# Mixture of experts on one core: the copies that take gathered rows apart and put them together move from GpSimd to ScalarE

## The chip, the cores and the metric

The kernel runs on one core of one Trainium2 chip. The metric is the device time of one execution in microseconds (us). Three runs of the kernel before are shown, 661.44, 663.84 and 665.75 us; a change is measured as the time after against the time before on one chip.

## What is computed

The reference is an attention over pooled keys and values, whose output feeds a layer of eight experts. Cut to what matters:

```python
k_p = k.reshape(B, H, Sp, 8, D).mean(axis=3); v_p = ...          # B, H, S, D = 8, 8, 576, 64
out = softmax(q @ k_p.T / 8) @ v_p                               # then x: 4608 tokens x 512
order = argsort(-(x @ w_gate).flatten())                         # 4608 x 8 gate values
for idx in order:                                                # greedy, 576 tokens for each expert
    tok, e = idx // 8, idx % 8
    if assigned[tok] < 0 and counts[e] < 576: assigned[tok] = e; counts[e] += 1
for e in range(8):
    out[assigned == e] = maximum(x[assigned == e] @ w1[e], 0) @ w2[e]     # 512 x 1024, 1024 x 512
```

## The kernel before, in words

**Two parts.** `Attention` takes the first 140 us or so and stores x (the tile `xd`, in DRAM). `experts` then works through the experts one after the other; the change is in this part. The experts are taken in the order in which the routing finds them full, and the routing of expert e+1 runs between the work of expert e.

**One expert.** 576 tokens are four tiles of 128 and one of 64. Products are made in three passes of rounded float32 parts: an operand is split into a high part, which ScalarE (ACT) makes by a copy to `fp32r`, and a low part, which VectorE (DVE) makes by a subtraction. So weights become `w1h`, `w1l` (L1034, L1038) and `w2h`, `w2l` (L1044, L1047), tokens `xh`, `xl` (L1026, L1027). `stage1` (L1064) makes h = x @ w1: first eight output tiles over tokens 0 to 255, then eight over tokens 256 to 575, twelve matmuls each (L1082), into five PSUM buffers `h`. ACT takes each finished tile to `hh` and, in the second half, `hr` (L1087, L1089), and DVE makes `hl` of the same PSUM tile (L1090); a buffer is free when both have read it. `stage2` (L1102) makes four tiles of 128 tokens with 24 matmuls each (L1116) and one of 64 (L1121). ACT copies each to `yt` (L1130, two buffers) or `yh`, and GpSimd (POOL) scatters it to the output by an indirect DMA (L1096).

**Getting an expert's tokens.** When the routing has the row numbers (`rows`, DVE, L740), `gather` (L975) fetches x by indirect DMAs on POOL (L997). For the first expert the tokens are turned by TensorE (PE) (L1058). For the other seven each tile goes through these steps:

- `fetch`: the rows of a tile land in one of the three places of `xa`;
- `split` (L1005): a copy on POOL takes the two 16-bit words of each float32 apart, from `xa` to `xg`, 1024 words on each partition;
- a DMA transpose on SP's queue (L1007) brings them back to `xa`, turned;
- `join` (L1014): a copy on POOL puts the two words together again, to `xg`;
- `xt_joined` (L1017): ACT makes `xh` of it and DVE `xl`.

Since `xa` has three places, tiles 3 and 4 are fetched when tiles 0 and 1 are joined. All fetches, splits and joins of an expert are issued in one stretch when the rows are known; POOL works through its queue in order, and so a scatter issued later waits behind them.

**The routing.** It is a search for the threshold of each expert: DVE makes comparisons (`cmp`, L601), PE counts them (`rt`, L644), DVE reduces, PE folds (L656), DVE compares (`g`, L663), PE spreads the answer (L670), and so on for four rounds, then `close` (L681) finds the rows. These PE instructions stand between the matmuls of the expert at work; PE works in order, so one that waits for DVE holds back the matmuls behind it.

**What sets the order of the work.** `experts` writes one program with a clock of its own, `now`, which counts the time that PE's matmuls should take. `advance` moves it on by the length of each matmul and issues the next step of the routing when the clock has come to it; `later` keeps DVE work until it is due; `turns` and `turn` issue `xt_joined` for tile t when 16 + 1.5 t us have passed on that clock since the rows. The engines keep the order that is written there, but not its times.

In this text the seven gatherings with splits and joins are numbered 1 to 7 by the expert that they are for. Gathering 1 falls into stage 2 of the expert before it, gathering 2 begins at the end of stage 1 of expert 1, and gatherings 3 to 7 begin in the middle of a stage 1.

Of the kernel before, what the change touches and what calls it, by code (L numbers as in the profile page):

```python
# [15 lines left out]
U16 = mybir.dt.uint16  # L16
AF = mybir.ActivationFunctionType
# [907 lines left out]
class Experts:  # L925
# [46 lines left out]
    def rows_of(self, t):  # L972
        return min(128, self.cap - 128 * t)

    def gather(self, rows, turned=False):  # L975

        self.xg = self.buf("xg", [128, 5, 512])
        if not turned:
            for t in range(5):
                self.fetch(rows, t, self.xg[:, t])  # L980
            return
        self.xa = self.buf("xa", [128, 3, 512])
        for t in range(3):
            self.fetch(rows, t, self.xa[:, t])
        for t in range(3):
            self.split(t)
        for t in range(5):
            self.join(t)
            if t < 2:
                self.fetch(rows, t + 3, self.xa[:, t])  # L990
            if t == 2:
                self.split(3)
                self.split(4)

    def fetch(self, rows, t, to):
        n = self.rows_of(t)
# [3 lines left out]
    def split(self, t):  # L1000

        nc = self.nc
        n = self.rows_of(t)
        xs = self.xg[:n, t].bitcast(U16)
        nc.gpsimd.tensor_copy(xs.rearrange("p (s d) -> p s d", s=2),  # L1005
                              self.xa[:n, t % 3].bitcast(U16).rearrange("p (d s) -> p s d", s=2))
        nc.sync.dma_start(self.planes(t), xs, transpose=True)  # L1007

    def planes(self, t):
# [1 line left out]

    def join(self, t):
        n = self.rows_of(t)
        self.nc.gpsimd.tensor_copy(self.xg[:, t].bitcast(U16).rearrange("p (j k s) -> p s j k", j=4, s=2)[:, :, :, :n],  # L1014
                                   self.planes(t).rearrange("p (s j) k -> p s j k", s=2))

    def xt_joined(self, t, later):  # L1017

# [127 lines left out]
def kernel(ctx, tc, q, k, v, wblk, moe_w1, moe_w2, out):  # L1146
# [23 lines left out]
    with ExitStack() as c2:  # L1170
        rows = cst.tile([128, 6], I32, name="lastrows")

        def keep():
            nc.vector.tensor_copy(rows[:, :5], R.rows)
            nc.vector.tensor_copy(rows[:, 5:], R.halves)


        X, flag, ps = experts(c2, tc, g, R, xd, moe_w1, moe_w2, out, A.ident, cap, keep)
        fast, X.scatters, X.fixed = X.scatters, [], True
        with tc.If(flag > 0):  # L1180
            experts_one_by_one(X, R, ps)
            keep()
        X.scatters += fast
        X.put(1, ps, rows, rows[:, 5:])
        for _ in X.stage2(7, rows, rows[:, 5:], range(2, 5)):
            pass


def experts(ctx, tc, g, R, xd, w1, w2, out, ident, cap, keep):
# [3 lines left out]
    nc = tc.nc  # L1193
    wk = ctx.enter_context(tc.tile_pool(name="moe", bufs=2))
    psB = ctx.enter_context(tc.tile_pool(name="psB", bufs=1, space=PSUM))
    X = Experts(tc, wk, psB, xd, w1, w2, out, ident, cap)

    toks, since, pieces, turned = {}, {}, {}, {}
    held, waiting = [], []

    now, dve, ready = 0.0, 0.0, 0.0

    def later(after, t, f):

        waiting.append((now + after, t, f))

    def flush(left=0):
        nonlocal dve
        while len(waiting) > left:
            due, t, f = waiting.pop(0)  # L1210
            f()
            dve = max(dve, due) + t

    def step(e):

        nonlocal now, ready, dve
        p, crit, t, what = held.pop() if held else next(g, (None, 0.0, 0.0, None))
        if p is None:
            return False
        if what == "id":  # L1220

            if p > e or p and pieces[p - 1].l < 8:
                held.append((p, crit, t, what))
                return False
            X.load_1(R.eid, 0, 4 if p else 2)
            eids[p] = R.eid
        elif what == "rows":
            if p and turned[p - 1] < 5:
                held.append((p, crit, t, what))
                return False  # L1230
            X.gather(R.rows, p > 0)
            toks[p] = R.rows, R.halves
            turned[p] = 0
        since[p, what] = now

        now += 0.2
        start = max(dve, now + 0.3)
        ready, dve = start + crit + 0.1, start + t
        return t > 0

    def advance(e, t):

        nonlocal now
        now += t
        while True:
            if waiting and waiting[0][0] <= now:
                flush(len(waiting) - 1)
            elif ready > now or not step(e):
                break

    def due(e, what, t):
        return (e, what) in since and now >= since[e, what] + t

    class Pieces:
# [10 lines left out]
        def next(self, ahead=True):  # L1265
            nonlocal dve
            if self.h == self.l:
                self.up()
            if ahead:
                self.up()  # L1270
            self.low(self.e, self.l)
            self.l += 1
            dve = max(dve, now) + 0.7
# [6 lines left out]
    def turn(e, t, name="tp", bufs=2):  # L1280

        nonlocal now
        if e:
            now = max(now, since[e, "rows"] + 16.0 + 1.5 * t)
            flush(1)
            X.xt_joined(t, later)
        else:
            now = max(now, since[e, "rows"] + 6.0 + 1.3 * t) + 0.45
            flush(1)
            X.xt(t, name, bufs, later)  # L1290
        turned[e] = t + 1
        if (e, t) == (0, 4):
            later(1.0, 0.2, lambda: X.load_2(behind(1)))

    def turns(e, upto, t0):

        nonlocal last
        t = turned.get(e, 5)
        if t < upto and due(e, "rows", 16.0 + 1.5 * t if e else 6.5 + 1.3 * t) and now >= last + 1.4:
            last = now  # L1300
            turn(e, t)

# [4 lines left out]
    while (0, "rows") not in since:  # L1307
        step(0)
# [3 lines left out]
    def behind(i):  # L1312
        nc.vector.tensor_copy(late[:, i:i + 1], eids[0])
        return late[:, i:i + 1]
# [10 lines left out]
    now = dve = -1.0  # L1325
    for t in range(2):
        turn(0, t)
        warm(2)
    flush()
    now, ready, dve = 0.0, 0.0, 1.0  # L1330
    last = 0.0
    for e in range(8):
# [5 lines left out]
        for n, dt in enumerate(X.stage1(later, not e)):  # L1338
            k = n if e else n - 48
            if 0 <= k < 48 and n % 2:  # L1340
                w1.by(4 + (k + 2) // 8)
            if (10 if e else 2) <= n < 96:
                turns(e, 5, n)
            if n == (84 if e else 40):
                for t in range(turned[e], 5):
                    turn(e, t)
            if n >= 64 and n % 2:
                w2.by((n - 70) // 14 if n > 70 else 0)
            if not more and n == 48:
                assert next(g, None) is None  # L1350
                flag = R.suspect()
                keep()
            elif not more and n == 136:
                flag = nc.values_load(flag[0:1, 0:1], min_val=0, max_val=1)
            advance(min(e + 1, 7), dt)
# [9 lines left out]
        if more:  # L1365
            while e + 1 not in toks:
                now = max(now, ready)
# [93 lines left out]
```

## Time and profile before

| | |
|---|---|
| runs shown | 661.44, 663.84, 665.75 us, median 663.84 |
| profiled execution | 658.44 us, of which the span is 656.3 us |
| mean granted TensorE clock | 0.956 of full speed |
| busy in the span | PE 597.4 us (91%), PE weight loads 515.1 (78%), DVE 446.8 (68%), POOL 258.3 (39%), ACT 237.3 (36%) |
| splits on POOL, L1005 | 35, the 28 of 128 partitions 1079 ns each |
| joins on POOL, L1014 | 35, the 28 of 1024 words 1443 ns each |
| indirect DMAs for rows, L997, of seven gatherings | 35, 995 ns each on POOL |
| chain of work that ended last | PE 49%, DVE 17%, POOL 16% of the span |

How to read it: the span runs from the first to the last instruction, and times in the timeline are counted from its start. A row of the timeline or of the groups names the line, the engine, the operation and its tiles, and in brackets how long the engine sat idle before it and what ended that. PE is busy for most of the time, so what counts is the time in which it is not, and the time in which its clock was granted at half speed.

### The profile page before, as it was taken

What the parts mean: (1) busy time and instruction counts of PE and PEld (TensorE: products, weight loads), DVE (VectorE), ACT (ScalarE), POOL (GpSimd) and SP (SyncE); (2) the same over time, 40 slices, a digit from 0 to 9 for tenths busy, and PEclk for the clock granted to TensorE, in tenths of its full rate; (3) what the DMA queues carried; (4) which work ended last, traced back from release to release, by engine and by line L of the source; (5) the groups of instructions that cost most, each with busy time, mean ns of one, the idle gap of its engine ahead of it and who ended that gap; (6) DMA issues with size and microseconds to landing.
All of it is one profiled execution on the core that took longest, in us unless ns stands there. A gap on an engine that the chain in (4) does not pass through costs nothing.

```text
span 656.3 us, 11241 instructions
## 1 busy us (share of the span) xinstructions
PE 597.4 (91%) x4155; PEld 515.1 (78%) x4155; DVE 446.8 (68%) x1149; ACT 237.3 (36%) x554; POOL 258.3 (39%) x289
## 2 busy tenths in 40 slices
PE   7999999976898779889799969997999899999994
PEld 5998989864896479669677967886789679988972
DVE  7677778888877568878974896499649916633400
ACT  7444444432532045134314423342225414524310
POOL 2999995002004710843622371146115522731011
PEclk9999999986999779899989999997999899999998
DMA  9999942125407343527411840283047218414011
GB/s 359 419 423 395 401 156 81 66 81 163 167 1 218 87 168 117 133 73 290 114 39 50 312 97 28 101 282 65 32 146 248 50 48 319 107 50 154 1 36 41
DMA packets 65985, 100.37 MB, mean 153 GB/s; under 512 B 36848, under 2 KB 36864, under 8 KB 63232
## 3 DMA queue, kind: packets, MB, share of 16 engines
q1 hardware_dynamic: 54672, 71.18, 32.3%
q0 software_dynamic: 5920, 18.89, 8.2%
q10 hardware_dynamic: 5328, 9.48, 3.8%
q8 instruction: 35, 0.57, 0.4%
q14 instruction: 30, 0.25, 0.1%
HBM read 72.40 MB, written 18.87 MB: 139 GB/s over the span
## 4 chain that ended last, share of the span: by engine, by line
PE 49%; DVE 17%; POOL 16%; issue 8%; DMA 6%; ACT 1%; SPq 1%; POOLq 0%; another core or an unknown queue 0%; DVEq 0%; ACTq 0%
PE h L1116 20%; PE h L1082 20%; DVE w2l L1047 4%; PE h L1121 3%; POOL t L187 3%; POOL tk L174 3%; DVE hl L1090 2%; DVE ow L574 2%; DMA rawk<-in_k_dram 2%; POOL kblk L178 2%; POOL t L188 2%; POOL vblk L197 2%; POOL tk L175 2%; PE psa L271 1%; DMA xa<-xg 1%
## 5 line engine op out<-in xcount | busy, mean ns | idle before, releaser
L1116 PE MATMUL h<-w2h,hh 128*128 128x512 f32 x256 | 103.6, 405 | 2.9 <-DVE hl L1090 2.6
L1116 PE MATMUL h<-w2h,hl 128*128 128x512 f32 x256 | 104.1, 407 | 0.0
L1116 PE MATMUL h<-w2l,hh 128*128 128x512 f32 x256 | 103.6, 405 | 0.0
L1087 ACT ACTIVATE hh<-h 128x320 fp32r<-128x320 f32 (+1 forms) x128 | 52.6, 411 | 140.6 <-PE h L1082 139.2
L1082 PE MATMUL h<-xh,w1h 128*128 128x320 f32 (+1 forms) x512 | 94.5, 305 | 4.1 <-ACT xh L1026 3.2
L1082 PE MATMUL h<-xl,w1h 128*128 128x320 f32 (+1 forms) x512 | 96.8, 306 | 0.0
L1096 POOL DMA_INDIRECT out_dram<-yt,rows x29 | 29.9, 1030 | 167.6 <-ACT yt L1130 166.7
L1082 PE MATMUL h<-xh,w1l 128*128 128x320 f32 (+1 forms) x512 | 93.5, 304 | 0.2 <-DVE w1l L1038 0.2
L1082 PEld LDWEIGHTS h<-xl,w1h 128*128 128x128 f32 x512 | 79.2, 196 | 9.2 <-issue 9.2
L1082 PEld LDWEIGHTS h<-xh,w1h 128*128 128x128 f32 x512 | 77.4, 194 | 7.9 <-ACT xh L1026 3.7
L1082 PEld LDWEIGHTS h<-xh,w1l 128*128 128x128 f32 x512 | 78.1, 195 | 0.6 <-DVE w1l L1038 0.5
L1130 ACT ACTIVATE yt<-h 128x512 f32<-128x512 f32 x32 | 19.2, 599 | 158.8 <-PE h L1116 97.9
L1090 DVE SCALAR_TENSOR_TENSOR hl<-h,hh 128x320 fp32r<-128x320 f32 (+1 forms) x128 | 56.9, 449 | 21.4 <-ACT hr L1089 13.7
L1027 DVE TENSOR_TENSOR xl<-xg,xh 128x512 fp32r<-128x512 f32 (+1 forms) x35 | 23.3, 665 | 64.3 <-ACT xh L1026 64.3
L997 POOL DMA_INDIRECT xa<-xd,rows x35 | 34.8, 995 | 75.4 <-DVE rows L740 67.3
L271 PE MATMUL psa<-vblk,eT 128*128 128x146 f32 (+3 forms) x400 | 62.0, 302 | 0.0
L1047 DVE TENSOR_TENSOR w2l<-raw,w2h 128x512 fp32r<-128x512 f32 x64 | 58.3, 919 | 2.2 <-ACT w2h L1044 2.1
L1116 PEld LDWEIGHTS h<-w2h,hh 128*128 128x128 f32 x256 | 49.6, 194 | 12.8 <-DVE hl L1090 2.9
L1014 POOL COPY xg<-xa 128x1024 uint16<-128x1024 uint16 (+1 forms) x35 | 46.8, 1348 | 26.8 <-DMA xa<-xg 26.7
L1116 PEld LDWEIGHTS h<-w2h,hl 128*128 128x128 f32 x256 | 49.7, 194 | 9.4
L1116 PEld LDWEIGHTS h<-w2l,hh 128*128 128x128 f32 x256 | 49.8, 195 | 9.1
L271 PEld LDWEIGHTS psa<-vblk,eT 128*128 128x128 f32 (+1 forms) x400 | 52.2, 180 | 1.7 <-issue 0.3
(215 smaller groups left out, 983.6 us busy)
## 6 DMA issues: line engine op xcount, KB each, us to landing
raw<-in_moe_w_dram SPq DMA_DIRECT2D x64, 512.0 KB, 6.7
xd<-xt ACTq DMA_DIRECT2D x36, 256.0 KB, 5.0
rawv<-in_v_dram SPq DMA_DIRECT2D x7, 1280.0 KB, 14.8
rawk<-in_k_dram SPq DMA_DIRECT2D x7, 1152.0 KB, 12.8
rawq<-in_q_dram SPq DMA_DIRECT2D x7, 1152.0 KB, 10.5
rawk<-in_k_dram SPq DMA_DIRECT2D x2, 576.0 KB, 4.4
rawv<-in_v_dram SPq DMA_DIRECT2D x1, 768.0 KB, 7.8
rawq<-in_q_dram SPq DMA_DIRECT2D x1, 640.0 KB, 8.9
```

The source lines that it names most:

```text
L174: eng.tensor_tensor(t1[:, c], src[:, c, :4], src[:, c, 4:], op=OP.add)
L187: eng.tensor_tensor(t1[:, c], src[:, c, :256], src[:, c, 256:], op=OP.add)
L271: self.nc.tensor.matmul(o[h], self.eT[i][:, c, h], self.vblk[b % 4][:, self.BLOCKS[c]:self.BLOCKS[c + 1]], start=(c == cs[0]), stop=(c == ...
L997: self.nc.gpsimd.indirect_dma_start(out=to[:n], out_offset=None, in_=self.xd, in_offset=bass.IndirectOffsetOnAxis(ap=rows[:n, t:t + 1], ax ...
L1014: self.nc.gpsimd.tensor_copy(self.xg[:, t].bitcast(U16).rearrange("p (j k s) -> p s j k", j=4, s=2)[:, :, :, :n], self.planes(t).rearrange ...
L1027: later(0.9, 0.7, lambda: self.nc.vector.tensor_tensor(xl, x, xh.bitcast(F32), op=OP.subtract))
L1047: self.nc.vector.tensor_tensor(self.w2l[:, i], self.raw2[e][:, i], self.w2h[:, i].bitcast(F32), op=OP.subtract)
L1082: nc.tensor.matmul(ps[:, :m], a[:, j, fs], b[:, j, o], start=(n == 0), stop=(n == 11))
L1087: nc.scalar.activation(hh[:, f, o], ps[:, :m], AF.Relu)
L1090: later(0.65, 0.4, lambda f=f, o=o, m=m, ps=ps: nc.vector.scalar_tensor_tensor(hl[:, f, o], ps[:, :m], 0.0, hh[:, f, o].bitcast(F32), op0= ...
L1096: st = nc.gpsimd.indirect_dma_start(out=rows, out_offset=bass.IndirectOffsetOnAxis(ap=idx, axis=0), in_=y, in_offset=None)
L1116: nc.tensor.matmul(ps, a[:, f, o], b[:, f], start=(f == 0 and k == 0), stop=(f == 7 and k == 2))
```

## The change

`split` and `join` become ACT copies (`activation` with `AF.Copy`) of the same words; the DMA transposes stay on SP and the fetches on POOL. `gather` no longer issues everything at once: it hands each split and join to `at`, which keeps it until the program's clock has come to a set time after the rows: splits 0 to 2 at 5.0, 6.3 and 7.6 us, joins 0 to 2 at 11.0, 12.3 and 13.6 us (joins 0 and 1 with the fetches of tiles 3 and 4 behind them), splits 3 and 4 at 16.9 and 18.2 us, joins 3 and 4 at 23.9 and 25.2 us. `advance` issues those that are due before it looks at the routing. `turn` comes 20 + 1.5 t us after the rows where it was 16 + 1.5 t. The first expert, and the second path through the experts that runs only if the routing's own test fails, keep the old fetch.

```diff
-    def gather(self, rows, turned=False):
+    def gather(self, rows, at=None):
...
         for t in range(3):
             self.fetch(rows, t, self.xa[:, t])
-        for t in range(3):
-            self.split(t)
-        for t in range(5):
-            self.join(t)
-            if t < 2:
-                self.fetch(rows, t + 3, self.xa[:, t])
-            if t == 2:
-                self.split(3)
-                self.split(4)
+            at(5.0 + 1.3 * t, lambda t=t: self.split(t))
+        for t in range(2):
+            at(11.0 + 1.3 * t, lambda t=t: (self.join(t), self.fetch(rows, t + 3, self.xa[:, t])))
+        at(13.6, lambda: self.join(2))
+        for t in range(3, 5):
+            at(13.0 + 1.3 * t, lambda t=t: self.split(t))
+        for t in range(3, 5):
+            at(20.0 + 1.3 * t, lambda t=t: self.join(t))
...
-        nc.gpsimd.tensor_copy(xs.rearrange("p (s d) -> p s d", s=2),
-                              self.xa[:n, t % 3].bitcast(U16).rearrange("p (d s) -> p s d", s=2))
+        nc.scalar.activation(xs.rearrange("p (s d) -> p s d", s=2),
+                             self.xa[:n, t % 3].bitcast(U16).rearrange("p (d s) -> p s d", s=2), AF.Copy)
...
-        self.nc.gpsimd.tensor_copy(self.xg[:, t].bitcast(U16).rearrange("p (j k s) -> p s j k", j=4, s=2)[:, :, :, :n],
-                                   self.planes(t).rearrange("p (s j) k -> p s j k", s=2))
+        self.nc.scalar.activation(self.xg[:, t].bitcast(U16).rearrange("p (j k s) -> p s j k", j=4, s=2)[:, :, :, :n],
+                                  self.planes(t).rearrange("p (s j) k -> p s j k", s=2), AF.Copy)
...
+    def at(after, f):
+
+        moves.append((now + after, f))
+
+    def move(until):
+        while moves and moves[0][0] <= until:
+            moves.pop(0)[1]()
...
-            X.gather(R.rows, p > 0)
+            X.gather(R.rows, at if p else None)
...
         now += t
+        move(now)
...
-            now = max(now, since[e, "rows"] + 16.0 + 1.5 * t)
+            now = max(now, since[e, "rows"] + 20.0 + 1.5 * t)
+            move(since[e, "rows"] + (11.0, 12.3, 13.6, 23.9, 25.2)[t])
...
-        if t < upto and due(e, "rows", 16.0 + 1.5 * t if e else 6.5 + 1.3 * t) and now >= last + 1.4:
+        if t < upto and due(e, "rows", 20.0 + 1.5 * t if e else 6.5 + 1.3 * t) and now >= last + 1.4:
```

The instructions change their places. In the rows below, line numbers of the changed kernel are its own: one less than before for the lines behind `gather` that the text names (the split is L1004, the join L1013, the scatter L1095, `yt` L1129). `x3` behind a row stands for three in a row.

POOL in gathering 1, before, from the first join on (`xg<-xa` are joins and splits, `out_dram` scatters):

```order
L1014 COPY xg<-xa 128x2x512
L997 DMA xa<-xd,rows 128x512
L1014 COPY xg<-xa 128x2x512
L997 DMA xa<-xd,rows 64x512
L1014 COPY xg<-xa 128x2x512
L1005 COPY xg<-xa 128x1024
L1005 COPY xg<-xa 64x1024
L1014 COPY xg<-xa 128x2x512
L1014 COPY xg<-xa 128x2x4x64
L1095 MEMSET spacer 1x1
L1096 DMA out_dram<-yt,rows 4608x512
```

POOL there now, from the three first fetches on:

```order
L996 DMA xa<-xd,rows 128x512 x3
L1094 MEMSET spacer 1x1
L1095 DMA out_dram<-yt,rows 4608x512
L1094 MEMSET spacer 1x1
L1095 DMA out_dram<-yt,rows 4608x512
L996 DMA xa<-xd,rows 128x512
L996 DMA xa<-xd,rows 64x512
L1094 MEMSET spacer 1x1
L1095 DMA out_dram<-yt,rows 4608x512
```

The scatters of expert 0's second and third tile now stand between the fetches; before, they stood behind the last join.

ACT at the same place, before (from expert 0's tiles of stage 2 to expert 1's first `xh`):

```order
L1130 ACTIVATE yt<-h 128x512 x3
L1034 ACTIVATE w1h<-raw_2602 128x512 x3
L1130 ACTIVATE yt<-h 128x512
L1034 ACTIVATE w1h<-raw_2602 128x512
L1026 ACTIVATE xh<-xg 128x4x128 x2
L1134 ACTIVATE yh<-h 128x256
L1034 ACTIVATE w1h<-raw_2602 128x512 x2
```

and now, from the third `yt` on (the three first splits stand right ahead of it):

```order
L1129 ACTIVATE yt<-h 128x512
L1033 ACTIVATE w1h<-raw_2602 128x512 x2
L1013 ACTIVATE xg<-xa 128x2x512
L1033 ACTIVATE w1h<-raw_2602 128x512
L1013 ACTIVATE xg<-xa 128x2x512 x2
L1129 ACTIVATE yt<-h 128x512
L1033 ACTIVATE w1h<-raw_2602 128x512
L1004 ACTIVATE xg<-xa 128x1024
L1004 ACTIVATE xg<-xa 64x1024
L1133 ACTIVATE yh<-h 128x256
L1033 ACTIVATE w1h<-raw_2602 128x512
L1025 ACTIVATE xh<-xg 128x4x128 x2
```

All five splits and three joins now stand ahead of the first `xh` on ACT, and so do `yh` and five pieces of `w1h` (four before).

ACT in the middle of expert 3's stage 1, where gathering 4 begins, before:

```order
L1044 ACTIVATE w2h<-raw_4392 128x512 x2
L1087 ACTIVATE hh<-h 128x256
L1044 ACTIVATE w2h<-raw_4392 128x512
L1087 ACTIVATE hh<-h 128x320
L1089 ACTIVATE hr<-h 128x64
L1044 ACTIVATE w2h<-raw_4392 128x512
L1087 ACTIVATE hh<-h 128x320
L1089 ACTIVATE hr<-h 128x64
```

and now:

```order
L1043 ACTIVATE w2h<-raw_4392 128x512 x2
L1004 ACTIVATE xg<-xa 128x1024
L1086 ACTIVATE hh<-h 128x256
L1043 ACTIVATE w2h<-raw_4392 128x512
L1004 ACTIVATE xg<-xa 128x1024
L1086 ACTIVATE hh<-h 128x320
L1088 ACTIVATE hr<-h 128x64
L1004 ACTIVATE xg<-xa 128x1024
L1043 ACTIVATE w2h<-raw_4392 128x512
L1086 ACTIVATE hh<-h 128x320
L1088 ACTIVATE hr<-h 128x64
```

The first split stands ahead of the last `hh` of the first half, and each later split or join between the evictions of two tiles.

More of the change, by code (lines that the diff above doesn't have):

```diff
@@ L973, in rows_of @@
         return min(128, self.cap - 128 * t)
-    def gather(self, rows, turned=False):
+    def gather(self, rows, at=None):
         self.xg = self.buf("xg", [128, 5, 512])
-        if not turned:
+        if at is None:
             for t in range(5):
@@ L1205, in later @@
         waiting.append((now + after, t, f))
+    moves = []
+    def at(after, f):
[3 more added lines that the diff above has]
+            moves.pop(0)[1]()
     def flush(left=0):
```

## The prediction

> **What bounds the kernel now.** I read the busy times of the page first, then PE's waits from 200 us on (us in total, times, the longest), then a table of stretches cut so that each of rows two to eight holds one gathering, 1 to 7.
>
> ```profile
> PE 597.4 (91%) x4155; PEld 515.1 (78%) x4155; DVE 446.8 (68%) x1149; ACT 237.3 (36%) x554; POOL 258.3 (39%) x289
> ```
>
> ```profile
> PE rt L644 <- DVE cmp L601: 13.1, 9, 3.2
> PE rt L670 <- DVE g L663: 9.0, 3, 3.4
> PE rt L656 <- DVE cnt L652: 3.7, 3, 1.3
> PE h L1082 <- ACT xh L1026: 3.2, 1, 3.2
> PE h L1116 <- DVE hl L1090: 2.6, 1, 2.6
> ```
>
> ```profile
> core 0: us, PE busy (x) PEld busy (x) DVE busy (x) ACT busy (x) POOL busy (x), PEclk, DMA share, GB/s
> 191.00:262.00 71.00, 61.81 (x400) 50.52 (x399) 49.30 (x141) 20.31 (x49) 21.39 (x24) 0.90 0.44 133
> 262.00:298.00 36.00, 32.39 (x190) 23.45 (x188) 29.41 (x81) 9.22 (x19) 22.19 (x24) 0.95 0.40 108
> 298.00:359.00 61.00, 56.08 (x380) 48.04 (x380) 46.73 (x117) 21.00 (x50) 22.55 (x25) 0.97 0.40 127
> 359.00:421.00 62.00, 56.18 (x380) 48.14 (x378) 45.91 (x114) 21.00 (x50) 21.89 (x25) 0.97 0.39 124
> 421.00:485.00 64.00, 58.17 (x390) 49.45 (x386) 45.97 (x114) 20.98 (x50) 21.70 (x25) 0.95 0.39 125
> 485.00:543.00 58.00, 54.77 (x341) 47.59 (x337) 37.84 (x82) 20.98 (x50) 22.26 (x25) 0.97 0.42 135
> 543.00:600.00 57.00, 57.00 (x379) 51.39 (x378) 29.73 (x61) 23.33 (x56) 24.21 (x26) 1.00 0.50 156
> ```
>
> PE bounds the kernel. What can be won is PE's idle time and the time its clock is granted at half. Length less PE busy gives 9.2, 3.6, 4.9, 5.8, 5.8, 3.2 and 0 us of idle; length times what PEclk lacks of 1 gives 7.1, 1.8, 1.8, 1.9, 3.2, 1.7 and 0. Together the gatherings lose 16.3, 5.4, 6.8, 7.7, 9.0, 4.9 and 0: **50.1 us is the most that this change can win** in them.
>
> The halved clock follows idle time. Columns here are PE's busy time, the granted clock, DMA share and GB/s:
>
> ```profile
> 271.40:274.80 3.40, 1.66 (x16) 1.00 0.51 95
> 274.80:278.20 3.40, 3.40 (x9) 0.50 0.24 84
> ```
>
> A stretch of 3.4 us in which PE is busy for less than half is followed by one at half clock, which costs 1.7 us. [...]
>
> Why DVE is late shows at 385 us. The rows are the timeline of DVE and POOL and two groups of DVE (ns min/median/max):
>
> ```profile
> 385.32 4.20 DVE L574 TENSOR_TENSOR ow<-oh,wts 128x288 f32<-128x288 bf16 x1
> 385.91 1.37 POOL L1014 COPY xg<-xa 128x1024 uint16<-128x1024 uint16 x1
> 387.19 2.01 POOL L1005 COPY xg<-xa 128x1024 uint16<-128x1024 uint16 x2
> L574 DVE TENSOR_TENSOR ow<-oh,wts x8: 436/1162/4201, 140.0 to 505.8; 128x288 f32<-128x288 bf16 x8
> L1090 DVE SCALAR_TENSOR_TENSOR hl<-h,hh x128: 402/448/492, 164.9 to 621.8; 128x256 fp32r<-128x256 f32 x64, 128x320 fp32r<-128x320 f32 x64
> ```
>
> `ow`, with both inputs in SBUF, takes 4.20 us where its fastest took 0.44, and ends when POOL's copies pause; `hl`, which reads PSUM, never stretches. So a POOL copy holds up DVE's instructions with two SBUF inputs. An indirect DMA alone doesn't:
>
> ```profile
> 371.29 0.95 POOL L997 DMA_INDIRECT xa<-xd,rows  x1 [0.31 <-issue]
> 371.83 0.44 DVE L779 TENSOR_TENSOR lg<-lg,pen 128x288 f32<-128x288 f32 x1
> ```
>
> Gathering 1 has a second loss. The scatters wait behind the joins on POOL, `yt` on ACT waits for a scatter, and `xh`, behind `yt`, lets PE begin expert 1 late:
>
> ```profile
> 203.35 1.01 POOL L997 DMA_INDIRECT xa<-xd,rows  x1 [3.17 <-DVE rows L740]
> 208.77 3.00 POOL L1005 COPY xg<-xa 128x1024 uint16<-128x1024 uint16 x3 [1.89 <-DMA xa<-xd,rows]
> 213.32 1.34 POOL L1014 COPY xg<-xa 128x1024 uint16<-128x1024 uint16 x1 [1.55 <-DMA xa<-xg]
> 230.35 0.60 ACT L1130 ACTIVATE yt<-h 128x512 f32<-128x512 f32 x1 [17.71 <-DMA out_dram<-yt,rows]
> 232.55 0.62 PE L1082 MATMUL h<-xh,w1h 128*128 128x256 f32 x3 [3.24 <-ACT xh L1026]
> ```
>
> **The price of a copy on ACT.** No row shows ACT copying 16-bit words with a stride. The nearest are these (busy us, mean ns):
>
> ```profile
> L447 ACT ACTIVATE j<-i 128x1152 f16<-128x1152 f32 x1 | 1.1, 1147 | 0.0
> L1044 ACT ACTIVATE w2h<-raw 128x512 fp32r<-128x512 f32 x64 | 38.9, 628 | 0.0
> L1005 POOL COPY xg<-xa 128x1024 uint16<-128x1024 uint16 x28 | 29.6, 1079 | 19.7 <-DMA xa<-xd,rows 16.8 <-ACT hr L1089 2.7
> L1014 POOL COPY xg<-xa 128x1024 uint16<-128x1024 uint16 x28 | 40.4, 1443 | 24.5 <-DMA xa<-xg 24.4
> ```
>
> 640 elements more cost 519 ns, so 0.81 ns each, and 1024 words cost 1.04 us. Lower bound: two words at a time, 0.63 us, the price of 512. Upper bound: twice the straight price, 2.1 us, if every strided word is paid double. I take 1.04, on the line between ACT's own two rows, and in a row 0.95, since neighbours overlap by about 0.1. An expert has ten copies, some 10 us; 70 us go from POOL (258 busy) to ACT (237). Over the whole span neither is near full; what matters is who waits behind a copy.
>
> **Gathering 1, step by step.** The first split still waits for the fetch, to 208.77; ACT's three end at 211.65. The first transpose lands about when it did, 213.2. Joins 0 to 2 end at 216.7 with one `yt` and three `w1h` around them. The fetch of tile 4, behind join 1 at 215.8, lands at some 220.1, so split 4, which stands ahead of `xh`, ends at 221.1; `yh`, a `w1h` and two `xh` follow, and PE begins expert 1 at about **223.0** (was 232.55). The scatters no longer stand behind joins, so `yt` finds its buffer. PE's own work of expert 0, without waits for `cmp`, ends at 221 to 222. Left: waits of 0.8 and 1.0 and one halved window, 1.7, together 3.5 of 16.3: **-12.8**.
>
> **Gathering 2** has DVE free and no ACT work near; 0.3 left of 5.4: **-5.1**.
>
> **Gatherings 3 to 5.** Here the change adds a wait. In gathering 4:
>
> ```profile
> 368.70 1.01 POOL L997 DMA_INDIRECT xa<-xd,rows  x1 [7.47 <-DVE rows L740]
> 375.55 3.05 POOL L1005 COPY xg<-xa 128x1024 uint16<-128x1024 uint16 x3 [3.31 <-DMA xa<-xd,rows]
> 372.33 0.39 ACT L1087 ACTIVATE hh<-h 128x256 fp32r<-128x256 f32 x1
> L1087 ACT ACTIVATE hh<-h 128x320 fp32r<-128x320 f32 x64 | 28.0, 438 | 82.0 <-PE h L1082 80.8 <-PE rt L755 1.2
> L1089 ACT ACTIVATE hr<-h 128x64 f32<-128x64 f32 x64 | 14.0, 218 | 0.0
> 380.72 0.39 PE L644 MATMUL rt<-oh,cmp 128*128 128x32 bf16 x9 [1.25 <-DVE cmp L601]
> 385.46 0.18 PE L656 MATMUL rt<-cnt,fold 128*128 128x8 f16 x1 [1.18 <-DVE cnt L652]
> 391.04 0.17 PE L670 MATMUL rt<-g,ones 128*128 128x8 bf16 x1 [3.39 <-DVE g L663]
> ```
>
> The rows take 6.85 us from issue to the first split. The first split stands on ACT ahead of the `hh` that ran at 372.33, so ACT stands still for some 3.3 us from 372.2, and that `hh` goes at 376.5. Behind it: `hl` on DVE (which needs `hh`), and behind `hl` the search. ACT then has eight copies (7.6), eight `hh` with their `hr` (3.6 with overlap) and seven `w2h` (3.7): 14.8 us, while PE makes eight tiles of 1.76 us, 14. So ACT catches up slowly, and the five PSUM buffers, some 7 us of PE, just cover it. DVE ends `cmp` at about 381.5 where PE stands at L644 from 379.47 (380.72 less 1.25): a wait of 2.1 where it was 1.25. The next ones have DVE unstretched: 0.35 at L656 (was 1.18), 0.25 at L670 (was 3.39), 1.2 at the next L644. That makes 3.9, and an even chance of a halved window 0.8: 4.7 left in each, of 6.8, 7.7 and 9.0: **-2.1, -3.0, -4.3**. If the buffers didn't cover ACT, its 3.3 us would fall on PE in each.
>
> **Gathering 6** has no search left, only `hl` late (L1116): 0.5 left of 4.9, **-4.4**. **Gathering 7** lost nothing; the copies beside its evictions **+0.5**. Moving `turn` by 4 us costs nothing, as PE reads those tokens only in the next stage 1, over 20 us on.
>
> Sum: -12.8 - 5.1 - 2.1 - 3.0 - 4.3 - 4.4 + 0.5 = **-31.2 us**; from the profiled 658.44 to 627.2. That execution is 0.8% under the median, so in the median 663.84 - 31.2 = 632.6, **633**.
>
> **Rivals.** *B, no new waits*: the rows land sooner in the changed order, or the buffers swallow ACT's stop (a copy at the lower bound takes 3.3 us of eight off ACT), and 3 x 4.7 = 14.1 more go: 619. For it, the fetch of gathering 1 landed after 5.4 us; against it, every gathering from 3 on took about 7. *C1, strided words cost on ACT what a join costs over a split on POOL*, 1.34 times: 1.4 us, 0.32 more for eight copies in five gatherings (1, 3 to 6), 13 us: 646. *D, DVE isn't freed*: POOL's indirect DMAs, which stay, hold it too. Only gathering 1's order gains, 9.6, less three waits longer by 0.85: 657. The row at 371.83 speaks against it, but only one DMA at a time is seen there. *C2, the slower side: ACT becomes the bound.* At 2.1 us a copy, eight copies cost 8.4 more in the half of stage 1 in which ACT already has 14.8 for PE's 14; with the buffers used up PE waits, 42 us in five gatherings against 31 won: 675. It decides from 31.2 / 40 = 0.78 above 1.04, that is at 1.8 us a copy. [...]
>
> **Chances.** Forecast 0.50, B 0.18, C1 0.13, D 0.09, C2 0.10. A measurement of this kernel, with runs 0.65% apart, can tell about 1%. The forecast, B and C1 are faster by over that, 0.81; D lies at its edge and counts as no change, 0.09; C2 is slower, 0.10. The range goes from B, with 2 us below, to D: 617 to 657.
>
> **What would show it.** Right: `ow` and `cmp` near 0.44 and 0.75 us throughout; no wait of `yt` for a scatter; PE's first stage-1 matmul of expert 1 near 223; the first split on ACT waiting some 3 us for its fetch in gatherings 3 to 6; PE's wait at L644 near 2 us there, those at L656 and L670 nearly gone; copies of 1.04 us. Wrong: stretched DVE instructions beside fetches (D), copies over 1.3 us or PE waiting for an `h` buffer (C1, C2), no wait ahead of the split (B).

## The result, and the profile after

The changed kernel takes **625.18 us** in the median of four runs (620.99 to 627.54), beside 664.8 us of the kernel before on the same chip (661.44 to 667.71). The ratio is **0.940, with a 95% interval of 0.933 to 0.947**. The forecast was 633, in a range of 617 to 657. The profiled execution took 625.91 us, with a span of 624.1 us.

The busy times of the page after:

```profile
PE 585.8 (94%) x4155; PEld 509.4 (82%) x4155; DVE 394.1 (63%) x1149; ACT 305.0 (49%) x624; POOL 175.3 (28%) x219
```

ACT has 68 us more and POOL 83 us less, as the moved copies make them. But DVE, whose 1149 instructions are the same, is busy 53 us less (it was 446.8): what it lost is time in which its instructions were held up. PE's 597.4 became 585.8, because fewer of its matmuls ran at half clock (the mean granted clock went from 0.956 to 0.973).

Of PE's waits from 190 us on, these are left (us in total, times, the longest):

```profile
PE rt L644 <- DVE cmp L601: 4.9, 3, 2.0
PE rt L670 <- DVE g L663: 2.2, 2, 1.1
PE h L1081 <- ACT xh L1025: 2.0, 1, 2.0
PE rt L656 <- DVE cnt L652: 0.8, 1, 0.8
```

In the kernel before they were 13.1, 9.0, 3.2 and 3.7, in this order, and one of 2.6 for `hl` at L1116 is gone. To see where the time came from, both traces are cut at the same places of the program: from the beginning of stage 2 of expert 0 to that of expert 1 (gathering 1), then to the beginning of stage 1 of expert 2 (gathering 2), and then from each stage 1 to the next (gatherings 3 to 6; gathering 7 has 52.05 us in both). The columns are length, PE's busy time, the granted clock, DMA share and GB/s. Before:

```profile
192.26:264.29 72.03, 62.84 (x406) 0.91 0.45 138
264.29:298.05 33.76, 30.15 (x174) 0.95 0.39 101
298.05:359.50 61.45, 56.52 (x383) 0.97 0.39 127
359.50:421.84 62.34, 56.52 (x383) 0.97 0.39 125
421.84:485.26 63.42, 57.59 (x383) 0.95 0.39 123
485.26:542.97 57.71, 54.48 (x338) 0.97 0.42 135
```

After:

```profile
195.91:256.83 60.92, 57.98 (x405) 0.97 0.55 168
256.83:284.79 27.96, 27.96 (x174) 1.00 0.43 110
284.79:342.41 57.62, 54.98 (x382) 1.00 0.43 136
342.41:400.64 58.23, 56.24 (x383) 0.97 0.44 134
400.64:458.16 57.52, 54.98 (x383) 1.00 0.45 135
458.16:510.75 52.59, 52.30 (x339) 1.00 0.47 148
```

Row by row, the gatherings give 11.1, 5.8, 3.8, 4.1, 5.9, 5.1 and 0 us, with unrounded rows 35.9. Stage 1 of expert 0 gives another 1.0 (31.19 to 30.20). Against that, the part ahead of it, which the change doesn't touch, took 161.07 us in the profile before and 165.71 after. In the profiles of the experiments below it ends anywhere from 160.8 to 165.6, so it belongs to the single execution. That takes 4.6 us off the difference, so the two profiled executions are only 32.5 us apart, and the medians 39.6.

DVE's group that stretched most before is even now (ns min/median/max), and `cmp`, up to 4.53 us before, takes 0.762 at most:

```profile
L574 DVE TENSOR_TENSOR ow<-oh,wts x8: 434/449/453, 144.5 to 479.0; 128x288 f32<-128x288 bf16 x8
```

The new wait is there too. First the timeline of gathering 4 on ACT, DVE and PE, then the two groups of copies on ACT (busy us, mean ns):

```profile
358.70 1.06 ACT L1004 ACTIVATE xg<-xa 128x1024 uint16<-128x1024 uint16 x1 [3.55 <-DMA xa<-xd,rows]
360.07 0.42 DVE L1089 SCALAR_TENSOR_TENSOR hl<-h,hh 128x256 fp32r<-128x256 f32 x1 [2.94 <-ACT hh L1086]
364.32 0.39 PE L644 MATMUL rt<-oh,cmp 128*128 128x32 bf16 x9 [1.99 <-DVE cmp L601]
```

```profile
L1004 ACT ACTIVATE xg<-xa 128x1024 uint16<-128x1024 uint16 x28 | 29.5, 1064 | 19.5 <-DMA xa<-xd,rows 18.6 <-DVE pen L777 0.9
L1013 ACT ACTIVATE xg<-xa 128x1024 uint16<-128x1024 uint16 x28 | 38.8, 1395 | 1.0 <-DMA xa<-xg 0.9
```

ACT stands 3.55 us for the fetch (2.94 to 3.25 in gatherings 3, 5 and 6), `hh` comes late, then `hl`, then the search on DVE, and PE waits 1.99 us. A split costs 1.06 us, a join 1.40.

### The profile page after: what moved, and what is told of

Read it like the earlier page. It is cut to its first block, busy times and chain, and to the rows that moved or that the text cites. A ratio compares the mean times of both kernels' runs of the same rounds, so it can differ in the third digit from the quotient of the medians.

```text
span 624.1 us, 11279 instructions
## 1 busy us (share of the span) xinstructions
PE 585.8 (94%) x4155; PEld 509.4 (82%) x4155; DVE 394.1 (63%) x1149; ACT 305.0 (49%) x624; POOL 175.3 (28%) x219
## 4 chain that ended last, share of the span: by engine, by line
PE 71%; issue 10%; DMA 7%; ACT 5%; DVE 3%; POOL 1%; POOLq 0%; another core or an unknown queue 0%; SPq 0%; DVEq 0%; ACTq 0%
PE h L1115 23%; PE h L1081 22%; PE psa L271 8%; PE pss L229 6%; DMA xa<-xd,rows 3%; PE h L1120 3%; PE pse L258 2%; ACT xg L1004 2%; PE rt L258 1%; DMA wblk<-in_moe_w_gate_dram 1%; DMA xg<-xd,rows 1%; PE rt L219 1%; PE rt L644 1%; ACT hh L1086 1%; PE rt L505 1%
## 5 line engine op out<-in xcount | busy, mean ns | idle before, releaser
L1115 PE MATMUL h<-w2l,hh 128*128 128x512 f32 x256 | 101.8, 398 | 0.0
L1115 PE MATMUL h<-w2h,hl 128*128 128x512 f32 x256 | 101.6, 397 | 0.0
L1115 PE MATMUL h<-w2h,hh 128*128 128x512 f32 x256 | 100.6, 393 | 0.3 <-PEq L1179 0.3
L1081 PE MATMUL h<-xl,w1h 128*128 128x320 f32 (+1 forms) x512 | 95.3, 303 | 0.0
L1081 PE MATMUL h<-xh,w1l 128*128 128x320 f32 (+1 forms) x512 | 91.0, 300 | 0.0
L1095 POOL DMA_INDIRECT out_dram<-yt,rows x29 | 29.2, 1006 | 200.0 <-ACT yt L1129 199.6
L1081 PEld LDWEIGHTS h<-xl,w1h 128*128 128x128 f32 x512 | 77.8, 192 | 2.3 <-issue 2.3
L1081 PEld LDWEIGHTS h<-xh,w1l 128*128 128x128 f32 x512 | 76.6, 192 | 0.1
L1129 ACT ACTIVATE yt<-h 128x512 f32<-128x512 f32 x32 | 19.2, 599 | 96.9 <-PE h L1115 62.5
L1115 PEld LDWEIGHTS h<-w2h,hl 128*128 128x128 f32 x256 | 48.2, 188 | 9.0
L1046 DVE TENSOR_TENSOR w2l<-raw,w2h 128x512 fp32r<-128x512 f32 x64 | 43.2, 682 | 5.8 <-ACT w2h L1043 5.8
L1004 ACT ACTIVATE xg<-xa 128x1024 uint16<-128x1024 uint16 (+1 forms) x35 | 36.8, 1064 | 19.7 <-DMA xa<-xd,rows 18.6
```

Source lines behind the costliest of these rows:

```text
L1004: nc.scalar.activation(xs.rearrange("p (s d) -> p s d", s=2), self.xa[:n, t % 3].bitcast(U16).rearrange("p (d s) -> p s d", s=2), AF.Copy)
L1046: self.nc.vector.tensor_tensor(self.w2l[:, i], self.raw2[e][:, i], self.w2h[:, i].bitcast(F32), op=OP.subtract)
L1081: nc.tensor.matmul(ps[:, :m], a[:, j, fs], b[:, j, o], start=(n == 0), stop=(n == 11))
L1095: st = nc.gpsimd.indirect_dma_start(out=rows, out_offset=bass.IndirectOffsetOnAxis(ap=idx, axis=0), in_=y, in_offset=None)
L1115: nc.tensor.matmul(ps, a[:, f, o], b[:, f], start=(f == 0 and k == 0), stop=(f == 7 and k == 2))
L1129: self.nc.scalar.activation(y, ps, AF.Copy)
```

## The experiments

Two theories were set against each other. S: the gain comes from POOL's copies no longer holding up DVE. O: it comes from the new order and times, whichever engine copies. Each kernel is the changed one with the edit shown; times are medians, ratios are against the kernel before on the same chip. Its medians lie between 663.4 and 664.8 us on the chips where times are compared, so times of two chips can be set side by side to within a microsecond or two.

### The new order, but on POOL

```diff
-        nc.scalar.activation(xs..., self.xa[:n, t % 3]..., AF.Copy)
+        nc.gpsimd.tensor_copy(xs..., self.xa[:n, t % 3]...)
```

and the same in `join`.

> The changed kernel with its splits and joins on POOL again, but issued where the plan's clock puts them. Theory S (the gain comes from POOL's copies no longer holding up DVE's instructions with two inputs in SBUF): ow, cmp and w2l stretch again, to 2 us and more, and only what gathering 1 wins by its scatters standing ahead of the joins stays: 645 to 658. Theory O (the gain comes from the new order and times, whatever engine copies): 625 to 630, with PE's waits as in the changed kernel.

Measured: **656.86 us, 0.986 (0.980 to 0.992)**. PE's waits, and a piece of DVE's and POOL's timeline:

```profile
PE rt L670 <- DVE g L663: 13.7, 5, 5.2
PE rt L644 <- DVE cmp L601: 6.5, 6, 1.9
PE rt L656 <- DVE cnt L652: 5.0, 4, 1.8
```

```profile
384.61 4.21 DVE L574 TENSOR_TENSOR ow<-oh,wts 128x288 f32<-128x288 bf16 x1
385.20 1.37 POOL L1013 COPY xg<-xa 128x1024 uint16<-128x1024 uint16 x1
386.48 2.02 POOL L1004 COPY xg<-xa 128x1024 uint16<-128x1024 uint16 x2
```

Theory O falls. With order and times kept, `ow` stands 4.21 us again, DVE is busy 452.2 us for 394.1, PE's waits at the search are 25.2 us for 7.9, and 31.7 of the 39.6 us are gone. The order by itself is worth 7 to 8 (664.12 to 656.86 on this chip).

### The new engine, but in one stretch

```diff
     def at(after, f):
-        moves.append((now + after, f))
+        f()
```

> The changed kernel with every split and join issued at once when the rows are known, as in the kernel before, but on ACT. If the plan's times are needed, ACT stands in its queue at the first split until the fetch lands, then at the joins until the transposes land, then at split 3 until the second fetches land: some 20 us for each gathering, of which the five PSUM buffers cover about 7. PE loses 10 us or more in six gatherings: 680 to 710, slower than the kernel before. If the engine alone matters, 625 to 632.

Measured: **751.32 us, 1.130 (1.124 to 1.136)**, worse than expected. ACT's waits:

```profile
ACT xg L1004 <- DMA xa<-xd,rows: 65.6, 16, 10.1
ACT xg L1013 <- DMA xa<-xg: 25.7, 15, 2.5
```

ACT stood 91 us for fetches and transposes, and the evictions, and all of DVE and PE behind them, stood with it: PE waits 88.7 us at stage 1 for `hl` alone. In the kernel before POOL stood in the same way, 26.7 us for transposes and 17.6 for fetches, but behind its copies stood only fetches and scatters, no evictions. So the engine is what gains, and the times are what makes the engine bearable.

### Copies on POOL that nobody waits for

```diff
         nc.scalar.activation(xs..., AF.Copy)
+        for _ in range(2):
+            self.nc.gpsimd.tensor_copy(self.scr..., self.scr...)
```

and the same in `join`; to make room for the tile `scr`, `yh` has one buffer where it had two. Nothing of the output depends on these copies.

> The changed kernel, and beside each split and join on ACT two copies of 512 words on POOL from a spare tile onto itself (yh has one buffer for two, to make room): about 1 us of POOL for each, 10 us a gathering, which nobody waits for. Theory S: DVE's instructions with two SBUF inputs stretch again beside them (ow, cmp, w2l to 1.5 us and more) and a good part of the 25 us that gatherings 2 to 6 won is lost again: 635 to 650. Theory O: POOL's copies are nobody's business, 625 within 3.

Measured: **629.33 us, 0.949 (0.944 to 0.954)**, 4 us above the changed kernel, with intervals that overlap: unclear by the time, and between the ranges of the two theories. `ow` went to 0.94 us at most. The second form took its words from `ident` with a stride for a split, and put them with a stride for a join:

```diff
+            self.nc.gpsimd.tensor_copy(self.scr...rearrange("p (r s d) -> p r s d", r=2, s=2), self.ident...rearrange("p (d s) -> p s d", s=2)...)
```

> As the run with idle copies on POOL, but each idle copy now takes 512 16-bit words from a constant (ident) with a stride, or puts them with a stride, as the real splits and joins did. In the first run of this kind the idle copies went from a tile onto itself without a stride, cost 4 us, and stretched ow to 0.94 us at most. If the stretch of DVE comes from POOL's copies as such, this run is like that one, 627 to 632, ow under 1 us. If it is the stride that makes POOL hold DVE up for the whole of its copy, ow and w2l go to 2 us and more and the time to 635 to 650.

Measured: **636.54 us, 0.961 (0.953 to 0.969)**, clear of the changed kernel, 11 us above it.

```profile
L574 DVE TENSOR_TENSOR ow<-oh,wts x8: 436/640/1017, 143.8 to 489.5; 128x288 f32<-128x288 bf16 x8
L1053 DVE TENSOR_TENSOR w2l<-raw,w2h x64: 668/685/1268, 182.8 to 588.8; 128x512 fp32r<-128x512 f32 x64
```

The time fell into the range of the second reading, but its sign didn't come: `ow` went to 1.02 us and `w2l` to 1.27, not to 2 and more. DVE was busy 428.7 us for 394.1, and PE waited 9.8 us at L644 for 4.9. So copies that nobody waits for do cost time through DVE, as theory S has it, but these held DVE up for one copy at a time, and they cost a third of what the real copies cost on POOL, although POOL was busy for longer (296.1 us, 259.6 with the real ones). PE's wait for `xh` also grew, from 2.0 to 3.4 us; whether the single `yh` buffer or the copies in front of scatters and fetches did that wasn't separated. The last two experiments look at how long DVE is held up.

### Only the splits, or only the joins, on POOL

The edit of the first experiment, in one of the two places (first in `split`, then in `join`):

```diff
-        nc.scalar.activation(xs..., self.xa[:n, t % 3]..., AF.Copy)
+        nc.gpsimd.tensor_copy(xs..., self.xa[:n, t % 3]...)
```

> The changed kernel with the splits on POOL again (5 of 1.08 us a gathering) and the joins on ACT, at the plan's times. Theory S (POOL's copies hold DVE up): DVE stretches during the splits alone, less than half of POOL's copy time of before; against that ACT no longer stands 3.5 us for the fetch: 625 to 638. If ACT's stop cost more than POOL's splits do, under 622.

> The changed kernel with the joins on POOL again (5 of 1.4 us a gathering) and the splits on ACT, at the plan's times. Theory S: the joins stretch DVE and ACT still stands 3.5 us for the fetch: 635 to 650, above the run with the splits on POOL. If only the splits hold DVE up, 622 to 628.

Measured: splits on POOL **624.81 us, 0.946 (0.937 to 0.954)**, not told apart from the changed kernel; joins on POOL **644.14 us, 0.974 (0.966 to 0.982)**. With the splits on POOL, POOL waits for the fetch in ACT's place (3.37 us in gathering 4), and what could be won by that seems to be paid back by splits beside DVE (PE waits 6.5 us at L644, 4.9 in the changed kernel).

With the joins on POOL, `w2l` has a mean of 914 ns (919 in the kernel before, 682 in the changed one):

```profile
L1046 DVE TENSOR_TENSOR w2l<-raw,w2h 128x512 fp32r<-128x512 f32 x64 | 58.1, 914 | 5.5 <-ACT w2h L1043 5.4
```

The first run, just under what S allowed, tells little, since two effects work against each other in it and were not separated. The second lies in S's range: joins on POOL cost 19 us.

### Every copy twice on ACT

```diff
         nc.scalar.activation(xs..., self.xa[:n, t % 3]..., AF.Copy)
+        nc.scalar.activation(xs..., self.xa[:n, t % 3]..., AF.Copy)
```

and the same in `join`, so that each is written twice to the same place.

> The changed kernel with every split and join on ACT made twice, to the same place: 12 us more of ACT in each gathering, as if a copy cost 2.1 us for a split and 2.8 for a join. This is the rival that ACT becomes the bound. If ACT had no room beside PE, its 9 us more in the half of stage 1 would fall on PE beyond what the five buffers still cover, 5 to 9 us in gatherings 1 and 3 to 6: 650 to 670. If ACT has room, 625 to 635.

Measured: **673.47 us, 1.020 (1.011 to 1.029)**: 9 us above the kernel before, and just above the range expected. PE's waits:

```profile
PE rt L670 <- DVE g L663: 16.6, 4, 4.6
PE rt L644 <- DVE cmp L601: 10.6, 4, 3.2
PE rt L656 <- DVE cnt L652: 9.1, 4, 4.2
PE h L1085 <- DVE hl L1093: 3.9, 4, 1.3
```

ACT's room is as small as the prediction had it, but it is hardly the five buffers that give out: only 3.9 us are spent waiting at stage 1 for `hl`. It is the search, with 36.3. DVE works in order, `hl` stands in front of `cmp`, `cnt` and `g`, and `hl` needs `hh` of the late ACT; PE waits at the three steps of the search.

### The due times later

All due times of gatherings 2 to 7, the turn too, 2.6 us later:

```diff
-            X.gather(R.rows, at if p else None)
+            X.gather(R.rows, (lambda a, f: at(a + LATE * (p > 1), f)) if p else None)
...
-            now = max(now, since[e, "rows"] + 20.0 + 1.5 * t)
+            now = max(now, since[e, "rows"] + 20.0 + LATE * (e > 1) + 1.5 * t)
```

`LATE` is 2.6.

> The changed kernel with the due times of gatherings 2 to 7 (splits, joins and the turn into xh) 2.6 us later, gathering 1 as it is. If what the change left in gatherings 3 to 5 is ACT standing at the first split until its fetch lands (3.55 us in gathering 4, and behind it hh, hl, cmp and PE's 1.99 us at L644), the first split now stands behind one or two more evictions, its wait falls from 3.5 to about 1 us, the three waits at L644 (1.49, 1.99, 1.38 us) go, and the time falls by 3 to 6 us, to 619 to 622. If ACT is the bound there by the sum of its work and not by that stop, the waits only come one tile later and the time stays at 625 within 2.

Measured: **617.73 us, 0.930 (0.926 to 0.934)**, 7.4 us under the changed kernel, more than expected. PE's waits, and what is left of ACT's for the fetch:

```profile
PE h L1081 <- ACT xh L1025: 2.0, 1, 2.0
PE rt L670 <- DVE g L663: 1.2, 3, 0.6
PE rt L644 <- DVE cmp L601: 1.0, 3, 0.3
...
ACT xg L1004 <- DMA xa<-xd,rows: 7.5, 6, 3.6
```

The longest wait left, 3.6 us, is that of gathering 1, which was not moved. In gatherings 2 to 7 the waits for fetches fell from 15.3 to 3.8 us, and PE's at L644 from 4.9 to 1.0. So it was the stop of ACT at the first split that the change had left in gatherings 3 to 5, and not the sum of ACT's work, which is the same here and hides. The run moves joins and turns with the splits, so the stop was not taken away alone. Then PE's single wait for `xh`, in gathering 1:

```diff
+def turn_at(e, t):
+    return 15.0 + 1.5 * t if e == 1 and t < 2 else 20.0 + LATE + 1.5 * t
```

with splits and joins 3 and 4 of gathering 1 2.6 us later.

> The run with gatherings 2 to 7 taken 2.6 us later, and in gathering 1 the turn of tokens 0 to 255 at 15.0 and 16.5 us, ahead of yh, with splits and joins of tiles 3 and 4 and the later turns 2.6 us later, behind it. What is left before the first expert after the first is PE's wait of 2.0 us for xh. If xh was late because two splits and yh stood ahead of it on ACT, that wait goes: 614 to 617, 2 us under the run it builds on (617.7). If the fetch and the transposes set it, it stays: 617 to 619.

Measured: **615.23 us, 0.926 (0.921 to 0.930)**. By time it isn't told apart from the one before it; in the trace the wait for `xh` is gone, and the same stretch is 2.3 us shorter (first the run it builds on, then this one):

```profile
191.29:251.33 60.04, 56.63 (x405) 1.00 0.55 172
```

```profile
197.11:254.88 57.77, 56.82 (x404) 1.00 0.55 171
```

It is the fastest kernel found here, 10 us under the changed one and 48 under the kernel before.

### The turn at 16 us again

```diff
-            now = max(now, since[e, "rows"] + 20.0 + 1.5 * t)
+            now = max(now, since[e, "rows"] + 16.0 + 1.5 * t)
```

and so in `turns`.

> The changed kernel with the turn into xh back at 16 us for 20. The step of the prediction that this move costs and wins nothing by itself: 624 to 628, unless the turn of tiles 3 and 4 then pulls joins 3 and 4 ahead of their due time, so that ACT stands for a transpose in front of evictions: 628 to 635.

Measured: **624.01 us, 0.940 (0.935 to 0.945)**, the same as the changed kernel. By the time, the later turn neither costs nor wins. In the trace it is not without effect: with the turn at 16 us the first two `xh` of gathering 1 stand ahead of `yh` on ACT, PE's wait of 2.04 us for them is gone, and the stretch of gathering 1 takes 57.6 us for 60.92, as short as in the run before this one. That the whole time doesn't show it may be due to waits elsewhere (at L670 3.4 us for 2.2) and to where the clock happens to be halved; this wasn't separated.

### What a copy costs, and what DVE does beside POOL

Work was added behind the end of the changed kernel, so its whole time says nothing:

```diff
+        for o, i in forms:
+            for t in range(4):
+                nc.scalar.activation(d16[t].rearrange(o, s=2), s16.rearrange(i, s=2), AF.Copy)
...
+            for t in range(3):
+                nc.gpsimd.tensor_copy(d16[t].rearrange(o, s=2), s16.rearrange(i, s=2))
...
+            for t in range(4):
+                nc.vector.tensor_tensor(xl[:, t], X.raw2[-1][:, t], X.w2h[:, t].bitcast(F32), op=OP.subtract)
```

Here `xl` is the tile `w2l`.

> The changed kernel with work added behind its end: 1024 16-bit words on 128 partitions copied four times each way (straight; read with a stride of two, as a split; written with a stride of two, as a join) by ACT, by DVE and by POOL, and then three copies of each kind on POOL beside four subtractions of DVE with both inputs in SBUF (128 x 512, alone 0.68 us). If the stride as such costs, read and written ones both take more than the straight one; if only the written stride costs, the first two agree at 1.05 us on ACT and the third takes 1.4. DVE beside POOL: the subtractions start only when POOL's three copies are through (one subtraction of 3 us or more), if POOL keeps DVE out for as long as its copies follow each other; each takes under 1.5 us if they take turns.

Measured on ACT, in the order straight, read with a stride, written with a stride, four each; then on POOL read and written:

```profile
614.15 3.88 ACT L1193 ACTIVATE xg<-xa 128x1024 uint16<-128x1024 uint16 x4
617.93 3.88 ACT L1193 ACTIVATE xg<-xa 128x1024 uint16<-128x1024 uint16 x4
621.71 4.89 ACT L1193 ACTIVATE xg<-xa 128x1024 uint16<-128x1024 uint16 x4
...
635.53 3.99 POOL L1199 COPY xg<-xa 128x1024 uint16<-128x1024 uint16 x4
639.46 5.02 POOL L1199 COPY xg<-xa 128x1024 uint16<-128x1024 uint16 x4
```

On both engines a stride of two in what is read cost nothing (3.88 us for four on ACT either way; on POOL 3.99 for four, where one straight copy, with DVE idle, took 1.04); a stride in what is written cost a quarter more (3.88 to 4.89, and 3.99 to 5.02, for four). That is most of the difference between split and join (1.06 and 1.40 us in the changed kernel). On DVE both cost: a straight copy took 0.43 us, one read with a stride 0.68, one written with a stride 0.73. Beside POOL's copies the subtractions took turns with them, two of 1.5 us for two copies of 1.5:

```profile
646.45 2.96 DVE L1207 TENSOR_TENSOR w2l<-raw,w2h 128x512 fp32r<-128x512 f32 x2
645.85 3.01 POOL L1204 COPY xg<-xa 128x1024 uint16<-128x1024 uint16 x2
```

That isn't what `ow` did in the kernel before, so one more run, again with work behind the end:

```diff
+        for k in range(3):
...
+            if k:
+                X.fetch(rows, 0, X.xa[:, k])
+            if k < 2:
+                for t in to:
+                    nc.gpsimd.tensor_copy(t, s16)
+            nc.vector.tensor_copy(small[:, 12:16], small[:, 0:4])
+            for t in range(4):
+                nc.vector.tensor_tensor(X.w2l[:, t], X.raw2[-1][:, t], X.w2h[:, t].bitcast(F32), op=OP.subtract)
```

`to` holds 1024 16-bit words each of the tiles `xg`, `raw` and `hr`.

> The changed kernel with work added behind its end: four subtractions of DVE with two inputs in SBUF (0.68 us alone) beside, first, three straight POOL copies to three tiles; second, the same three behind an indirect DMA of POOL; third, an indirect DMA alone. In the run that added prices DVE and POOL took turns, and a subtraction took 1.5 to 1.75 us, where ow in the kernel before stood 4.2 us through an indirect DMA and three copies. If it is the indirect DMA in front of the copies that lets POOL keep DVE out, the second part shows a subtraction of 3 us or more and the first and third don't. If it is that the copies go to tiles of their own, the first shows it too. If none shows it, what made POOL keep DVE out for three copies stays open.

Measured, first the part without a DMA (the first and the third of its copies), then that behind one (DVE, then POOL's third copy), then the DMA alone:

```profile
614.38 1.03 POOL L1198 COPY xg<-xa 128x1024 uint16<-128x1024 uint16 x1
614.48 2.91 DVE L1199 COPY small<-small 128x4 f32<-128x4 f32 x1 [23.99 <-POOL small L1193]
616.33 1.03 POOL L1198 COPY hr<-xa 128x1024 uint16<-128x1024 uint16 x1
...
621.43 3.90 DVE L1201 TENSOR_TENSOR w2l<-raw,w2h 128x512 fp32r<-128x512 f32 x1
623.74 1.04 POOL L1198 COPY hr<-xa 128x1024 uint16<-128x1024 uint16 x1
...
626.38 1.89 DVE L1201 TENSOR_TENSOR w2l<-raw,w2h 128x512 fp32r<-128x512 f32 x3
626.80 1.12 POOL L996 DMA_INDIRECT xa<-xd,lastrows  x1 [0.54 <-issue]
```

The 4 us of `ow` are there again. Three copies in a row kept DVE out to the end of the third: without the DMA a small copy of DVE for 2.91 us (0.17 with no copy beside it), and with the indirect DMA in front a subtraction for 3.90. The DMA alone stretched nothing (three subtractions in 1.89 us). So POOL's copies do it, not its DMAs. Why DVE got a turn between the copies in the run before and not here stays open: copies to tiles of their own went through in one go here, but the copies of the kernel before go to one tile and did so too.

## Why the prediction was right, point by point

**The cause** was right in each of its links. POOL's copies hold DVE up (shown by the run with the new order on POOL, +31.7 us, and by the run of copies that nobody waits for, +11 us), PE waits for DVE at the search (its waits at L644, L656 and L670 fell from 25.8 to 7.9 us), and the halved clock follows (17.5 us lost in the gatherings before; after, 0.03 of 60.92 and of 58.23, some 3.6). The hold-up shows on some of DVE's instructions and not on others: `hl`, which reads PSUM, took 0.49 us at most in the kernel before and in the changed one, beside POOL's copies too (in the kernel before 0.48 at 380.59, within a join that ran from 379.95 to 381.88), while the subtraction of two SBUF tiles took 3.90 us behind three copies of the last experiment, where its median in the changed kernel is 0.68. In all it was worth 32 us of 664.

**Gathering 1**: -12.8 predicted, -11.1 measured. PE began expert 1 20.6 us after the first fetch (207.00 to 227.62), where 19.65 were expected (203.35 to 223.0). The joins took 1.37 us where 0.95 were expected, and yet the last split ended only 0.24 us late (17.99 us after the first fetch, 17.75 expected). What held `xh` up last was `yh`, which stands ahead of it on ACT and waited for the last product of expert 0 on PE:

```profile
225.62 0.38 ACT L1133 ACTIVATE yh<-h 128x256 f32<-128x256 f32 x1 [0.63 <-PE h L1120]
```

So PE waited 2.04 us for `xh`, where the sum had 1.0. Here the step "Moving `turn` by 4 us costs nothing, as PE reads those tokens only in the next stage 1, over 20 us on" doesn't hold: in gathering 1 PE reads them at once, and the later turn put `xh` behind `yh`. The two runs that put it ahead of `yh` have no such wait.

**Gathering 2**: -5.1 predicted, -5.8 measured. **Gatherings 6 and 7**: -4.4 and +0.5 predicted, -5.1 and 0 measured.

**Gatherings 3 to 5** were the step that was mis-sized: -2.1, -3.0, -4.3 predicted, and -3.8, -4.1, -5.9 measured. The new wait came where it was expected: ACT 3.55 us at the first split of gathering 4 (3.3 predicted), PE at L644 1.49, 1.99 and 1.38 us (2.1 predicted). What was sized too large is what follows it: 1.8 us of later waits in each, where two of the three have 1.09 at L670 and nothing else, and 0.8 for halved clock in each, where one of the three had it (clock 0.97 in gathering 4, some 1.7 us). DVE, no longer held up, made up its lateness faster than the sum had it: none of the three shows a wait at L656 or at the next L644.

**The price of a copy**: 1.04 us was right for a split (1.06) and too low for a join (1.40). That is nearly rival C1's ratio (1.31 beside 1.34), for one of the two kinds, and its sign, copies over 1.3 us, came for the joins. Its 13 us didn't come, and neither did its other sign: no wait of PE for an `h` buffer shows in the changed kernel, so ACT still had room there. The 70 us that were to go from POOL to ACT leave out the copies of the small tiles: POOL lost 83 us, and ACT got copies of 81 us, which overlap with their neighbours, so that its busy time grew by 68.

**B** (no new waits) did not come by itself: the rows landed no sooner (6.82 to 7.15 us from the first fetch to the first split in gatherings 3 to 6, 6.85 to 7.41 before). It came when the due times were put behind the landing, 617.7 where B had 619. **D** (DVE isn't freed) falls: the changed kernel has all its indirect DMAs on POOL, among them 35 fetches of rows and 29 scatters of `yt`, and its eight `ow` take 0.453 us at most and `cmp` 0.762; beside the lone DMA of the last experiment no subtraction was stretched. **C2** (copies twice as dear) was measured by doubling them: 673.5 where it had 675. The agreement is luck: the doubled copies made ACT busy for 11 us more in each of seven gatherings (382.9 us in all for 305.0), where C2 had 8.4 in five, and PE hardly runs out of `h` buffers, as C2 had it; it waits at the search. That ACT becomes the bound at such a price is right.

**The sum** was -31.2. The gatherings gave 35.9 and stage 1 of expert 0, on which nothing was forecast, 1.0. The remaining 2.7 us to the 39.6 between the medians lie within what the first 161 to 166 us differ from run to run; that they come from there isn't shown.

## What to carry to other kernels

When instructions of one engine have very different times for the same shape (0.44 and 4.20 us), look at what another engine did meanwhile before you look at that engine: here copies on GpSimd, which was busy for only 39% of the span, set the time of PE through VectorE. Moving such copies to an engine that evicts needs a due time behind the landing of their data, since an engine that works in order turns each early issue into a stop: on ACT at once 751 us, at the times of the change 625, 2.6 us later 618. And of what a change leaves over, the first new wait in each stage tells where to go on.

## What had not been expected of the hardware

- On ACT a copy of 1024 16-bit words costs the same whether it is read straight or with a stride of two (3.88 us for four), and a quarter more if it is written so (4.89; in the kernel a join took 1.40 beside a split's 1.06). On POOL it is the same (a straight copy 1.04 us; 3.99 for four read with a stride, 5.02 written). On DVE a strided read costs too (0.68 for 0.43 us).
- It isn't only DVE's instructions with two SBUF inputs that POOL's copies hold up, as the prediction had it: a copy of 128x4 float32, with one, stood for 2.91 us where it takes 0.17 alone.
- The same wait of 2.04 us for `xh` was followed by some 1.7 us lost at halved clock in the changed kernel (clock 0.97 over 60.92 us) and by none in the one with later due times (1.00 over 60.04 us). So how long PE idles doesn't settle alone whether the clock is halved.
